# Layer 1's plain slices in six blocks of 384 tokens, attention's queries in parts of 384 and 192, the order drawn with lengthened durations

## The chip, the core and the metric

The kernel runs on one core of a Trainium2 chip. The metric is the device time of one execution in microseconds. The engines are TensorE (PE in the rows; PEld is its loading of weights), VectorE (DVE), ScalarE (ACT), GpSimd (POOL) and SyncE (SP), which issues all DMAs.

## What is computed

Attention with a threshold over 4 batches, 8 heads, 576 tokens and 64 channels, and behind it two feed-forward layers on the 2304 tokens it gives, each with an inner width of 2048:

```python
scores = scale * np.matmul(q, k.transpose(0, 1, 3, 2))
thresh = np.max(scores, axis=-1, keepdims=True) - tau
scores = np.where(scores >= thresh, scores, -1000000000.0)
attn = np.exp(scores - np.max(scores, axis=-1, keepdims=True))
attn = attn / (np.sum(attn, axis=-1, keepdims=True) + 1e-09)
x = np.matmul(attn, v)                          # to (2304, 512)
h = x @ w_in                                    # layer 1, 512 to 2048
g = np.where(h >= 1, h, np.where(h <= -1, 0.0, (h + 1) ** 2 / 4))
x = g @ w_out                                   # 2048 to 512
h = x @ w_in2                                   # layer 2
y = (s * np.maximum(h, 0) ** 2 + b) @ w_out2
```

All data are fp32, and the weights come in as fp64. Products that need the precision are done as three fp32r matmuls with a high and a low part of each factor.

## The kernel before

The program is not written in the order in which it runs. Functions `add` tasks (some instructions on one engine, or on one of several) with a duration, a priority and the buffers that they read and write; `Sched.run` plays them through with these durations and writes every engine's instructions in the order in which they began there. Each engine then works through its own list in that order and waits where a semaphore isn't set. Where the planner sees PE idle before `FILL` (200 us of its own clock) and a bank is free, it puts in a dummy matmul of the identity (L1541), which computes nothing that is used.

The work has three stages. **Attention** takes 32 units, a pair of heads and one part of a batch's queries each; a part was 256 queries (two blocks of 128 rows) or 320 (two blocks, and a mixed one with the last 64 queries of both heads). For each block of 128 queries of one head ("head-block" below): scores on PE (L587 in plain fp32 for the first two batches, L596 in fp32r from the third on), min on VectorE (L640), exp on ScalarE (L643) into a tile `p`, threshold and sum on VectorE (L648), division (L683, L678), transposes on PE (L704, L720) and their evictions (L696) into `pt` and `pl`. A tile `p` holds two head-blocks, and there are `NP` = 4 of them. When a unit's blocks are there, `av` multiplies them by the values (L742, L743): one value product for each unit, evicted into `xh` and `xl`, high and low part, and copied to `xT` in DRAM.

**Plain slices** are layer 1's first 8 of 16 slices of 128 inner channels. The tokens lay in eight blocks, two to a batch, of 256 and 320 tokens. For a block and a slice, `hidden` multiplies 12 matmuls (L937), ScalarE and VectorE shape the result (L943 to L949, L565), and `a1_out` (L970) or `l1_out` (L1018) multiplies 12 more for the output. `FB` says how many slices of a block run beside attention, as lower priority in between: 3, 7, 8, 8, 8, 8, 8 of the first seven blocks. The others (8 of the last block, 5 of the first, 1 of the second) follow attention. Weights are converted from fp64 in pieces on ScalarE, VectorE and GpSimd while attention starts.

**Passes**: the other half of layer 1, and layer 2, in three passes over three blocks of 768 tokens with a scheme that saves multiplications (`gemm1` and what follows it; L1275, L1320, L1394, L1436).

Scores use pairs of PSUM banks, three pairs up to unit `ALONE` and two from there on, when the third becomes the two banks of the slices.

Of the kernel before, what the change touches and what calls it, by code (L numbers as in the profile page):

```python
# [1 line left out]

# [5 lines left out]
F32 = mybir.dt.float32  # L8
# [16 lines left out]
FB = [3, 7, 8, 8, 8, 8, 8]  # L25
# [13 lines left out]
NP, NST, NH, LEAD = 4, 4, 3, 3  # L39
NYS = 8  # L40
# [13 lines left out]
ALONE = 7  # L54
# [40 lines left out]
HELD = float("inf")  # L95

# [33 lines left out]
class Sched:  # L130
# [241 lines left out]
def attention_then_ffn(tc, qk, v, tau, w1, w2, s2, b2, out):  # L372
# [198 lines left out]
    def scores(u, blk, x):  # L571
# [126 lines left out]

    def blocks_of_keys(u, pr, p, kp, c0, x, mixed, blk):
# [14 lines left out]
        dst = PT[:, :, :, 512:S].rearrange("p s k c -> p k s c") if mixed else PT[:, x, :, blk * 128:blk * 128 + 128]  # L714
        evict(512, pr, [dst], src, [("bank", g)], kt, g)

    def last_keys(u, pr, p, kp, mixed, blk):

        g = Group([(4,), (5,)])
        add([("pe", 109, lambda: nc.tensor.transpose(bank[g.banks[0]][:, 0:128], p[:, 512:640], ident))], at(pr, "trans"), r=kp, w=[("bank", g)] + [("PL", blk)] * (u < ALONE), group=g)  # L720
# [5 lines left out]
        c = slice(512, S) if mixed else slice(blk * 128, blk * 128 + 128)  # L726
        evict(300 if mixed else 128, pr, [PL[0:64, c], PL[64:128, c]] if mixed else [PL[:, c]], src, [("bank", g)], [("PL", blk)], g)

    def av(u, b, pair, part):
# [4 lines left out]
        c0, n = ((0, 256), (256, 320))[part]  # L734
        blks = ((0, 1), (2, 3, 4))[part]
# [59 lines left out]
    def attention():  # L795
# [8 lines left out]
        for u, (b, pair, half_) in enumerate(units):  # L804
# [3 lines left out]
            if pair == H // 2 - 1 and 2 * b + half_ < NA1:  # L808
                beside(2 * b + half_)
# [807 lines left out]
```

## Time and profile before

| | us |
|---|---|
| median of 3 runs | 1058.02 (1057.4 to 1058.94) |
| the profiled execution | 1057.3 |
| its span, first to last instruction | 1055.2 |
| PE busy | 1032.3 (98%) |
| VectorE, ScalarE, GpSimd busy | 866.8, 729.4, 493.5 |
| end of the slices, start of the passes | 502.29 |

PE is the busiest engine, but a PE record lasts longer than the step from one matmul to the next, since matmuls are pipelined; where a matmul's price matters, it is read from the chain, which counts steps, or from one start to the next. The granted clock is 1.00 of 2.4 GHz in all stretches.

### The profile page before, as it was taken

How to read it: one execution, taken by the hardware profiler on the slowest of the kernel's cores; microseconds unless marked ns; L12 is line 12 of the kernel's file. 1: busy time of each engine (PE TensorE's matmuls, PEld its weight loads, DVE VectorE, ACT ScalarE, POOL GpSimd, SP SyncE). 2: the span in 40 equal slices, each digit the busy share in tenths (PEclk: the TensorE clock that was granted, in tenths of full speed). 3: DMA queues.
4: the chain of work that ended last, by engine and by line, in shares of the span. 5: the costliest groups of instructions: out<-in, count | busy, mean ns of one | idle time of the engine just before them, and what ended most of it. 6: DMA issues, size and time to landing. Idle time of an engine off the chain costs nothing.

```text
span 1055.2 us, 20159 instructions
## 1 busy us (share of the span) xinstructions
PE 1032.3 (98%) x6772; PEld 931.7 (88%) x6772; DVE 866.8 (82%) x1786; ACT 729.4 (69%) x1418; POOL 493.5 (47%) x722
## 2 busy tenths in 40 slices
PE   8989999999999999999999999999999999999998
PEld 5556777788888889899999999998998989999998
DVE  7998998778888888755998978789998636988887
ACT  7999988988899889844553635358685636647381
POOL 5665766899998878523101513222231103424241
PEclk9999999999999999999999999999999999999999
DMA  5654555565656666389965659974968946445531
GB/s 175 184 171 147 152 171 178 168 208 159 215 160 215 198 193 206 119 288 378 343 197 208 200 194 377 333 254 161 338 224 310 381 151 208 152 133 194 174 101 61
DMA packets 117943, 221.01 MB, mean 209 GB/s; under 512 B 12752, under 2 KB 37072, under 8 KB 117840
## 3 DMA queue, kind: packets, MB, share of 16 engines
q1 hardware_dynamic: 117840, 219.73, 62.7%
q8 instruction: 54, 0.88, 0.4%
q14 instruction: 49, 0.40, 0.1%
HBM read 152.44 MB, written 67.24 MB: 208 GB/s over the span
## 4 chain that ended last, share of the span: by engine, by line
PE 71%; ACT 14%; DVE 7%; POOL 4%; issue 3%; DMA 1%; SPq 0%; POOLq 0%; DVEq 0%; ACTq 0%
PE ps L1275 25%; PE ps L1320 9%; PE ps L1436 9%; PE ps L1394 9%; ACT p L683 4%; PE ps L937 4%; PE ps L970 4%; ACT p L643 3%; PE ps L742 3%; ACT pt L696 2%; DVE p L648 2%; PE ps L1018 2%; PE ps L704 2%; PE ps L587 1%; DVE stt L640 1%
## 5 line engine op out<-in xcount | busy, mean ns | idle before, releaser
L1275 PE MATMUL ps<-pr,lr 128*128 128x384 f32 x816 | 144.2, 334 | 0.0
L1275 PEld LDWEIGHTS ps<-pr,lr 128*128 128x128 f32 x816 | 141.7, 188 | 0.0
L648 DVE SCALAR_TENSOR_TENSOR p<-ps,stt,p 128x576 f32<-128x576 f32 x144 | 115.4, 813 | 30.4 <-ACT p L643 24.7
L1275 PE MATMUL ps<-lr 128*128 128x384 f32 x672 | 121.1, 334 | 0.0
L1275 PEld LDWEIGHTS ps<-lr 128*128 128x128 f32 x672 | 116.8, 188 | 0.2
L640 DVE TENSOR_REDUCE stt<-ps 128x1 f32<-128x576 f32 x144 | 105.8, 748 | 10.4 <-PE ps L587 6.3
L937 PE MATMUL ps<-xh,lr 128*128 128x320 f32 (+1 forms) x512 | 112.2, 299 | 1.9 <-DVE lf L947 0.8
L643 ACT ACTIVATE p<-ps,stt 128x576 f32<-128x576 f32 x144 | 104.4, 746 | 7.2 <-DVE stt L640 6.3
L683 ACT ACTIVATE p<-p,stt 128x576 f32<-128x576 f32 (+3 forms) x127 | 101.7, 811 | 6.5 <-DVE stt L667 5.0
L566 DVE TENSOR_TENSOR pr<-lg,pr 128x768 fp32r<-128x768 f32 (+1 forms) x79 | 69.9, 904 | 33.3 <-PE ps L1436 17.2
L937 PEld LDWEIGHTS ps<-xh,lr 128*128 128x128 f32 x512 | 84.8, 188 | 4.2 <-DVE lf L947 2.3
L970 PE MATMUL ps<-g,lr 128*128 128x256 f32 (+1 forms) x600 | 87.1, 297 | 0.5 <-ACT lf L979 0.4
L704 PE MATMUL ps<-ident,p 128*128 128x128 f32 x576 | 82.5, 275 | 4.5 <-ACT pt L696 3.0
L1162 ACT COPY lg<-ps 128x384 f32<-128x384 f32 (+1 forms) x106 | 51.7, 491 | 50.5 <-PE ps L1275 38.9
L970 PEld LDWEIGHTS ps<-g,lr 128*128 128x128 f32 x600 | 80.4, 188 | 1.6 <-ACT lf L979 0.8
L704 PEld LDWEIGHTS ps<-ident,p 128*128 128x128 f32 x576 | 66.2, 140 | 17.2 <-ACT pt L696 4.1
L696 ACT COPY pt<-ps 128x512 f32<-128x512 f32 x140 | 78.3, 589 | 4.4 <-PE ps L704 4.0
L1436 PE MATMUL ps<-lr,pr 128*128 128x512 f32 x324 | 76.5, 389 | 0.0
L937 PE MATMUL ps<-xl,lr 128*128 128x256 f32 (+1 forms) x256 | 75.2, 294 | 0.0
L742 PE MATMUL ps<-pt,vr 128*64 128x256 f32 (+1 forms) x512 | 69.4, 412 | 3.1 <-DVE lf L947 2.5
L1436 PEld LDWEIGHTS ps<-lr,pr 128*128 128x128 f32 x324 | 60.8, 188 | 12.5
L565 POOL TENSOR_TENSOR g<-lf,g 128x256 fp32r<-128x256 f32 (+1 forms) x64 | 53.9, 844 | 35.2 <-ACT g L949 32.1
(155 smaller groups left out, 2470.4 us busy)
## 6 DMA issues: line engine op xcount, KB each, us to landing
lr<-wd SPq DMA_DIRECT2D x178, 256.0 KB, 5.3
wd<-lh SPq DMA_DIRECT2D x102, 256.0 KB, 3.8
lk<-in_w_dram SPq DMA_DIRECT2D x48, 512.0 KB, 4.9
vr<-in_v_dram SPq DMA_DIRECT2D x32, 320.0 KB, 3.4
r<-in_qk_dram SPq DMA_DIRECT2D x32, 288.0 KB, 3.1
lg<-y1T SPq DMA_DIRECT2D x6, 1536.0 KB, 8.2
lk<-in_w_dram SPq DMA_DIRECT2D x32, 256.0 KB, 3.8
wd<-pr SPq DMA_DIRECT2D x28, 256.0 KB, 4.3
```

The lines of the kernel that those rows point to most:

```text
L640: add([("dve", 665, lambda: nc.vector.tensor_reduce(out=nm[:, x:x + 1], in_=Sv(), axis=AX.XY, op=ALU.min))], at(pr, "min"), r=[kg], w=[ks[ ...
L643: add([("act", 624, lambda: nc.scalar.activation(out=ev, in_=Sv(), func=AF.Exp, bias=nm[:, x:x + 1], scale=-1.0))], at(pr, "exp"), r=[kg, ...
L648: nc.vector.scalar_tensor_tensor(out=ev, in0=Sv(), scalar=nthr[:, x:x + 1], in1=ev, op0=ALU.is_le, op1=ALU.mult, accum_out=sm[:, x:x + 1])
L683: nc.scalar.activation(out=p[i:j, o:o + w], in_=p[i:j, a:a + w], func=AF.Identity, scale=rc[i:j, x:x + 1], bias=un[i:j, x:x + 1])
L696: add([("act", actp_ns(n), lambda: [nc.scalar.copy(out=a, in_=b) for a, b in zip(dst, src())]), ("dve", dve_ns(n), lambda: [nc.vector.tens ...
L704: nc.tensor.transpose(bank[g.banks[0]][:, j * 128:(j + 1) * 128], p[:, c0 + j * 128:c0 + (j + 1) * 128], ident)
L742: nc.tensor.matmul(o[64 * x:64 * x + 64, 0:n], vr[:, c:c + D], PT[:, x, k, c0:c0 + n], start=(k == 0), stop=False)
L937: nc.tensor.matmul(o, a, x, start=(n == 0), stop=(n == 11))
L970: nc.tensor.matmul(o, a[:, c], x, start=(f == 0 and n == 0), stop=(f == nf - 1 and n == 2))
L1275: nc.tensor.matmul(o, a, y, start=(i == 0 and p in (1, 5, 2)), stop=(i == 5), skip_group_check=p not in (1, 5, 2))
L1320: nc.tensor.matmul(o, w, x, start=(f == rows[0] and s == 0), stop=(f == rows[-1] and s == 2))
L1436: nc.tensor.matmul(o, a, y, start=(f == rows[0] and s == 0), stop=(f == rows[-1] and s == 2))
```

## The change

- The tokens of two batches make three blocks of 384: the first 384 of one batch, the last 192 of both, the first 384 of the other. So there are six blocks, and `FB` has five entries: 4, 8, 8, 8, 8. Four slices of block 0 and eight of block 5 follow attention.
- A unit has 384 queries (three blocks of 128) or 192 (one block and the mixed one). In batches 1 and 3 the parts of 192 come first, so that a block of two pieces is complete early. `pt` and `pl` shrink to 384 columns, two parts of 192 side by side.
- `hidden` is two tasks of six matmuls, between which the planner may put something else (`HK`). The output was in two parts already.
- While its clock is below 460 us, the planner lengthens each duration on ScalarE, VectorE and GpSimd by a random 0 to 10% (seed `DRAW`).
- `NP` is 3 for 4, `NYS` 5 for 8, `ALONE` 6 for 7.

```diff
+HK = 2
+AK = 2
+
+TM = 384
+NQ = NT // TM
 WC = 256
 NWT = 4
 
-FB = [3, 7, 8, 8, 8, 8, 8]
+FB = [4, 8, 8, 8, 8]
...
-NP, NST, NH, LEAD = 4, 4, 3, 3
-NYS = 8
+NP, NST, NH, LEAD = 3, 4, 3, 3
+NYS = 5
...
-ALONE = 7
+ALONE = 6
...
+DRAW, SPREAD, DRAW_TO = 3, 0.1, 460000.0
...
+                    if now < DRAW_TO and e in ("act", "dve", "pool"):
+                        t.fn = (e, t.fn[1] * (1.0 + SPREAD * rnd.random()), *t.fn[2:])
...
+    YE = [ap_.tile([128, TM], F32, name=f"ye{i}") for i in range(2)]
...
-        return (0 if half_ else 256), nk, (nk if half_ else 0), (256 if not half_ else 320 if b < SPLIT else 384)
+        return (0 if half_ else TM), nk, (nk if half_ else 0), (TM if not half_ else S - TM if b < SPLIT else 256)
...
+    def col(u, blk):
+
+        return 128 * blk if not units[u][2] else (S - TM) * (units[u][1] % 2) + 128 * (blk - 3)
+
+    def pt_keys(x, c, n):
+        return [(x, i) for i in range(c // 64, (c + n) // 64)]
...
-        c0, n = ((0, 256), (256, 320))[part]
-        blks = ((0, 1), (2, 3, 4))[part]
+        n = S - TM if part else TM
+        c0 = col(u, 3 * part)
...
-    units = [(b, pair, half_) for b in range(B) for half_ in range(2) for pair in range(H // 2)]
...
+    units = [(b, pair, half_) for b in range(B) for half_ in ((1, 0) if b % 2 else (0, 1)) for pair in range(H // 2)]
+
+    def block_of(b, part):
+        return 3 * (b // 2) + (1 if part else 2 * (b % 2))
+
+    def pieces(q):
+
+        b = 2 * (q // 3)
+        return [(b * S + TM, S - TM), (b * S + S + TM, S - TM)] if q % 3 == 1 else [(b * S + S * (q % 3 // 2), TM)]
...
-        for part, blks in ((0, (0, 1)), (1, (2, 3))):
+        for part, blks in ((0, (0, 1, 2)), (1, (3,))):
...
-            if pair == H // 2 - 1 and 2 * b + half_ < NA1:
-                beside(2 * b + half_)
+            if pair == H // 2 - 1 and (b % 2 or not half_) and block_of(b, half_) < NA1:
+                beside(block_of(b, half_))
...
+        def mm(ks):
...
+        for i in range(0, 4, HK):
+            ks = range(i, i + HK)
+            add([("pe", 3 * HK * mm_ns(T), lambda ks=ks: mm(ks), "r")], pr, r=["two"] + wkeys(f, 0) + [(t, xs, j, a) for t in ("XH", "XL") for j in range(4) for a in range(2)], w=[kg, "hidden order"] + gs[0] + gs[1], group=g)
...
+            fs = range(half_ * nf // AK, (half_ + 1) * nf // AK)
...
-    blocks = [(q, 0, F1) for q in range(NA1, 2 * B)]
+    blocks = [(q, 0, F1) for q in range(NA1, NQ)]
```

What this makes of the order is seen on PE. The first place is around the 11th value product. In before, behind it (`ps_1_1128` and its like are a bank, `p_104` a tile of probabilities, `r_112` queries and keys of one head):

```order
L587 MATMUL ps_0_94<-r_112 128x288 x2
L587 MATMUL ps_1_95<-r_113 128x288 x2
L704 MATMUL ps_0_96<-ident,p_104 128x128 x4
L720 MATMUL ps_1_97<-ident,p_104 128x128
L1541 MATMUL ps_1_1128<-ident 128x128 x7
L704 MATMUL ps_0_96<-ident,p_105 128x128 x4
L587 MATMUL ps_0_94<-r_112 128x288 x2
L704 MATMUL ps_1_97<-ident,p_105 128x128 x4
L720 MATMUL ps_0_96<-ident,p_105 128x128
L587 MATMUL ps_1_95<-r_113 128x288 x2
```

And in the changed kernel, between the 10th and the 11th value product, where the lines are L1582 for the dummies, L719 and L738 for the transposes, L595 for the scores:

```order
L719 MATMUL ps_0_98<-ident,p_104 128x128 x4
L719 MATMUL ps_1_99<-ident,p_104 128x128 x4
L1582 MATMUL ps_1_1212<-ident 128x128 x12
L738 MATMUL ps_0_98<-ident,p_104 128x128
L1582 MATMUL ps_1_1212<-ident 128x128 x2
L719 MATMUL ps_1_99<-ident,p_105 128x128 x4
L595 MATMUL ps_0_96<-r_115 64x288 x2
L595 MATMUL ps_0_96<-r_116 64x288 x2
L738 MATMUL ps_0_98<-ident,p_105 128x128
L595 MATMUL ps_1_97<-r_113 128x288 x2
L1582 MATMUL ps_1_1212<-ident 128x128
L760 MATMUL ps_0_1211<-pt,vr_117 64x192 x8
```

Seven dummies stood in one run before, and 39 in the whole program; now one run has twelve, and there are 93, 92 of them ahead of the 12th value product. No slice stands in that stretch of the changed kernel.

The second place is in the third batch. Before, a hidden slice stood in one piece between transposes and scores:

```order
L720 MATMUL ps_0_96<-ident,p_103 128x128
L704 MATMUL ps_1_97<-ident,p_104 128x128 x4
L937 MATMUL ps_0_1127<-xh_73,lr 128x256
L937 MATMUL ps_0_1127<-xl_75,lr 128x256
L937 MATMUL ps_0_1127<-xh_73,lr 128x256 x2
L937 MATMUL ps_0_1127<-xl_75,lr 128x256
L937 MATMUL ps_0_1127<-xh_73,lr 128x256 x2
L937 MATMUL ps_0_1127<-xl_75,lr 128x256
L937 MATMUL ps_0_1127<-xh_73,lr 128x256 x2
L937 MATMUL ps_0_1127<-xl_75,lr 128x256
L937 MATMUL ps_0_1127<-xh_73,lr 128x256
L596 MATMUL ps_0_94<-lr 128x288 x4
```

Now (L978 is the hidden slice, L760 and L761 the value product):

```order
L978 MATMUL ps_1_1212<-xh_74,lr 128x384
L978 MATMUL ps_1_1212<-xl_76,lr 128x384
L978 MATMUL ps_1_1212<-xh_74,lr 128x384 x2
L978 MATMUL ps_1_1212<-xl_76,lr 128x384
L978 MATMUL ps_1_1212<-xh_74,lr 128x384
L760 MATMUL ps_0_1211<-pt,vr_117 64x192 x8
L761 MATMUL ps_0_1211<-pl,vr_117 128x192
L738 MATMUL ps_0_98<-ident,p_104 128x128
L719 MATMUL ps_1_99<-ident,p_105 128x128 x4
L978 MATMUL ps_1_1212<-xh_74,lr 128x384
L978 MATMUL ps_1_1212<-xl_76,lr 128x384
L978 MATMUL ps_1_1212<-xh_74,lr 128x384 x2
```

Six matmuls of a slice stand alone, then a value product and transposes, then the other six of the same sum.

## Rows read from the trace of the kernel before

**Rows 1.** Windows: length, busy PE, PEld, DVE, ACT, POOL; clock, DMA share, GB/s.

```profile
0.00:50.00 50.00, 44.14 (x284) 28.32 (x286) 42.30 (x107) 42.07 (x84) 29.35 (x74) 1.00 0.61 184
50.00:100.00 50.00, 45.07 (x321) 29.99 (x317) 45.50 (x120) 46.84 (x101) 30.42 (x64) 1.00 0.50 157
0.00:150.00 150.00, 139.05 (x953) 95.26 (x953) 134.63 (x344) 134.27 (x283) 96.13 (x205) 1.00 0.55 165
150.00:500.00 350.00, 341.25 (x2539) 301.59 (x2536) 275.77 (x665) 287.02 (x583) 261.98 (x373) 1.00 0.64 206
450.00:500.00 50.00, 49.43 (x363) 47.76 (x362) 28.23 (x55) 21.40 (x49) 16.72 (x19) 1.00 0.96 339
```

**Rows 2.** Chain that ended last, pieces in order of time: start, us, what.

```profile
21.36 1.88 PE ps L742 x16
...
28.32 0.69 PE ps L587 x4
...
71.55 2.30 PE ps L742 x16
...
74.59 0.44 PE ps L704 x4
...
138.19 1.88 PE ps L742 x16
...
142.56 1.56 PE ps L1541 x14
...
204.18 2.80 PE ps L970 x24
...
455.53 7.08 PE ps L937 x48
...
502.29 28.09 PE ps L1275 x162
```

**Rows 3.** The same chain from 0 to 150 us, shares by line.

```profile
by line: PE ps L742 11.8%; PE ps L937 10.4%; PE ps L587 9.8%; ACT p L683 9.5%; PE ps L704 8.9%; ACT pt L696 7.4%; ACT p L643 6.9%; PE ps L1541 5.3%; DMA lk<-in_w_dram 4.4%; issue 3.9%; PE ps L743 3.9%; ACT lk L879 2.1%; DVE stt L640 1.4%; D
```

**Rows 4.** Timeline of PE: start, us, instructions in a run, idle before and releaser.

```profile
1.34 2.50 PE L790 MATMUL ps<-ident 128*128 128x128 f32 x10 [1.34 <-POOL ident masks.py:199]
...
7.13 2.39 PE L1541 MATMUL ps<-ident 128*128 128x128 f32 x18
9.46 1.24 PE L587 MATMUL ps<-r 64*128 64x288 f32 x8
...
14.08 0.33 PE L720 MATMUL ps<-ident,p 128*128 128x128 f32 x1 [0.63 <-ACT pt L696]
...
23.17 0.70 PE L743 MATMUL ps<-pl,vr 128*128 128x256 f32 x2
23.70 0.60 PE L704 MATMUL ps<-ident,p 128*128 128x128 f32 x4
24.23 1.24 PE L587 MATMUL ps<-r 64*128 64x288 f32 x8
...
73.78 0.81 PE L743 MATMUL ps<-pl,vr 128*128 128x320 f32 x2
74.43 0.60 PE L704 MATMUL ps<-ident,p 128*128 128x128 f32 x4
...
289.67 0.78 PE L596 MATMUL ps<-lr 128*128 128x288 f32 x4
...
290.83 0.27 PE L720 MATMUL ps<-ident,p 128*128 128x128 f32 x1
```

**Rows 5.** Groups of instructions by form: busy us, mean ns of one, idle before.

```profile
L1541 PE MATMUL ps<-ident 128*128 128x128 f32 x78 | 12.4, 292 | 1.4 <-ACT pt L696 1.0 <-ACT lf L979 0.4
...
L945 ACT ACTIVATE lf<-lf,cst 128x320 f32<-128x320 f32 x32 | 17.9, 564 | 13.9 <-DVE lf L943 13.7
...
L945 ACT ACTIVATE lf<-lf,cst 128x256 f32<-128x256 f32 x32 | 16.2, 507 | 3.1 <-DVE lf L943 3.0
```

**Rows 6.** Timeline of ScalarE: the first two exps.

```profile
6.38 1.45 ACT L643 ACTIVATE p<-ps,stt 128x576 f32<-128x576 f32 x2
```

More of the change, by code (lines that the diff above doesn't have):

```diff
@@ L719, in last_keys @@
         g = Group([(4,), (5,)])
-        add([("pe", 109, lambda: nc.tensor.transpose(bank[g.banks[0]][:, 0:128], p[:, 512:640], ident))], at(pr, "trans"), r=kp, w=[("bank", g)] + [("PL", blk)] * (u < ALONE), group=g)
+        at_, m = col(u, blk), 64 if mixed else 128
+        kl = pt_keys("PL", at_, m)
+        add([("pe", 109, lambda: nc.tensor.transpose(bank[g.banks[0]][:, 0:128], p[:, 512:640], ident))], at(pr, "trans"), r=kp, w=[("bank", g)] + kl * (u < ALONE), group=g)
         def src():
@@ L743, in mm @@
             nc.tensor.matmul(o[:, 0:n], vr[:, 8 * D:8 * D + 128], PL[:, c0:c0 + n], start=False, stop=True)
-        rd = ["two"] * (u >= ALONE) + [("VR", u % NV)] + [("PT", x, t) for x in range(2) for t in blks] + [("PL", t) for t in blks]
-        q = 2 * b + part
-        t0, c = b * S + c0, slice(pair * n, pair * n + n)
-        xh, xl, kh, kl = XH[q % 2][:, c], XL[q % 2][:, c], ("XH", q % 2, pair), ("XL", q % 2, pair)
-        add([("pe", value_ns(n), mm)], at(pr, "av"), r=rd, w=[kg, kh, kl], group=g)
+        rd = ["two"] * (u >= ALONE) + [("VR", u % NV)] + [k for t in ("PT0", "PT1", "PL") for k in pt_keys(t, c0, n)]
@@ L751, in av @@
+        q, parts = block_of(b, part), (b % 2,) if part else (0, 1)
+        t0, c = b * S + TM * part, pair * TM + (S - TM) * (part and b % 2)
+        xh, xl = XH[q % 2][:, c:c + n], XL[q % 2][:, c:c + n]
+        kh, kl = ([(t, q % 2, pair, a) for a in parts] for t in ("XH", "XL"))
+        add([("pe", value_ns(n), mm)], at(pr, "av"), r=rd, w=[kg] + kh + kl, group=g)
         add([("act", actp_ns(n), lambda: nc.scalar.copy(out=xh, in_=bank[g.banks[0]][:, 0:n])),
              ("dve", dve_ns(n), lambda: nc.vector.tensor_copy(out=xh, in_=bank[g.banks[0]][:, 0:n]))],
-            at(pr, "xo"), r=[kg], w=[kh], group=g)
+            at(pr, "xo"), r=[kg], w=kh, group=g)
@@ new lines, in columns, with shaped_as, among, x_keys @@
+    def columns(t, q):
+        b = 2 * (q // 3)
+        if q % 3 == 1:
+            return t[:, b * S:b * S + 2 * S].rearrange("p (a c) -> p a c", a=2)[:, :, TM:S]
+        return t[:, pieces(q)[0][0]:pieces(q)[0][0] + TM]
+    def shaped_as(y, q):
+        return y.rearrange("p (a c) -> p a c", a=2) if q % 3 == 1 else y
+    def among(t0, T):
+        return [q for q in range(NQ) if any(a < t0 + T and a + w > t0 for a, w in pieces(q))]
+    def x_keys(qs, x):
+        return [("xT", q, p, x, a) for q in qs for p in range(H // 2) for a in range(2)]
@@ L1179, in load_x @@
         keys = [("y1", t0, dm, a) for dm in range(4) for a in ((0,) if dm < 3 or T <= 512 else (0, T // 2))]
-        qs = [q for q in range(2 * B) if span(q)[0] < t0 + T and sum(span(q)) > t0]
+        qs = among(t0, T)
         if P.layer == 1:
-            keys = [("xT", q, p, 0) for q in qs for p in range(H // 2)]
+            keys = x_keys(qs, 0)
         add([("sp", DMA_ISSUE, lambda: nc.sync.dma_start(out=x_b(0, 4 * T).rearrange("p (k t) -> p k t", k=4), in_=rows_of(src)))],
@@ L1304, in gemm2_across @@
         rows = P.rows()
-        qs = [q for q in range(2 * B) if span(q)[0] < t0 + T and sum(span(q)) > t0]
+        qs = among(t0, T)
         def at_(dm, a):
@@ L1485, in hid @@
         q, f0, _ = blocks[k]
-        T = span(q)[1]
+        T = TM
         gs[n] = gslot(n % NGL, T)
         hidden(f, T, (k + NA1) % 2, ANY, gs[n])
-        if f == f0 + 1 and 2 * B - NA1 <= k + 1 < len(blocks):
+        if f == f0 + 1 and NQ - NA1 <= k + 1 < len(blocks):
             load_parts(blocks[k + 1][0], (k + 1 + NA1) % 2)
```

100 lines of the change are left out of this document (48 added, 52 removed).

## The prediction

> **What bounds the kernel now.** I read the table of windows first [rows 1]; the reader is to see how little of TensorE (PE) is free. It is idle for 150 - 139.05 = 10.9 us up to 150 us, mostly in the first 100, and for 350 - 341.25 = 8.8 us from there to 500: in all 19.7. At 50 to 100 us ScalarE has 46.84 and VectorE 45.50 of 50 busy, PE 45.07: attention runs nearly alone there and nobody is idle for long.
>
> Then the chain that ended last [rows 2]. From 502.29 us on it is matmuls of the passes, to the end of the span (1055.2): 552.9 us, which the change doesn't touch. From 455.53 to 502.29 it is slices alone, dense. So everything is decided before 502.29, and before that by what PE has to do and what it waits for. The third view is the share of the lines in the chain up to 150 us [rows 3]: 5.3% of it, 8.0 us, are matmuls of L1541, the dummies that the planner puts where its own plan shows PE idle. They take their time on the path, and whatever stands behind them waits.
>
> **A ledger of PE up to 502.29 us.** A slice's matmul takes 2.80 / 24 = 0.1167 us for 256 tokens and 7.08 / 48 = 0.1475 for 320 [rows 2]; 768 of each make 89.6 + 113.3 = 202.9. A value product takes 1.88 us (256 queries) or 2.30 (320), and its last matmul 0.53 or 0.65 (23.17 to 23.70, 73.78 to 74.43) [rows 2, 4]: 16 of each, 66.9 + 18.9. Transposes: 0.44 for four [rows 2], so 656 x 0.11 = 72.2. Scores in plain fp32: 0.69 a group of four records [rows 2], 80 groups, 55.2. Scores in fp32r: eight in 1.16 us (289.67 to 290.83) [rows 4], 320 of them, 46.4. Dummies: 18 records from 7.13 to 9.46, 0.129 each [rows 4]; there are 78 records (39 matmuls) [rows 5], 10.1. Warm-up 2.5 [rows 4]. Sum 475.1; **the rest**, 27.2 us, is the 19.7 of idle time and 7.5 of switches and waits too short to show.
>
> **The change part by part.**
>
> Six blocks of 384. A matmul of 384 tokens stands in the passes: 28.09 / 162 = 0.1734 us [rows 2]. 1152 of them make 199.7: **-3.2 us**. The gain is that a token costs 0.451 ns at 384 against 0.456 and 0.461. The Trainium skill (TensorE: Matmul & The Clock Gate, section Back-to-back issue gap) has a rule that speaks for less: a warm gap of N / 2.4 ns plus a fixed 2.5. By it only 384 fixed parts would go, the term would be -1.0 and the sum end at 1057, no change. The rows differ from it (0.1167 where it gives 0.109), and the sum goes by the rows.
>
> Where the slices lie moves too. Before, 27 slices of 256 and 23 of 320 run beside attention, 75.6 + 81.4 = 157.0 us, and 45.9 are left. Now 36 of 384 run beside it (149.8) and 12 after it (49.9). That is in the -3.2 already; it says only that the dense stretch at the end grows by 4.0.
>
> Queries in 384 and 192. Value products are linear between the two rows, 0.42 us for 64 queries, so 2.72 + 1.46 = 4.18, as 1.88 + 2.30 before; the last matmuls likewise. Scores, transposes, exps, masks and evictions are as many as before. **Nothing**. The ACT and DVE work of the slices falls with their number, 64 to 48: the square takes 564 ns for 320 and 507 for 256 [rows 5], so 279 ns of it don't depend on the width, and 16 x 0.28 = 4.5 us leave ScalarE, beside PE. It shortens waits at most; if ScalarE were the bound it would be a gain of up to 4.5, and I leave it out.
>
> DMAs: xT and ypT go out in as many bytes, a block of two pieces in two loads. The DMA share is 0.55 up to 150 us, and 0.96 from 450 to 500 [rows 1], but the slices there follow each other without a wait. So nothing, as long as the loads of block 0 come before its turn; 8 slices of block 5 (33 us) lie ahead of it on PE. Without that cover a load would cost what it takes to land, a few us.
>
> The third pair of banks for scores is given up one unit earlier (`ALONE` 6 for 7): three head-blocks with one score less in flight, between nothing and about 1 us (the length of a score and its min), nearer to nothing because slices stand in the same banks then.
>
> Slices in two turns. A hidden slice may be left after six matmuls. A switch to fp32 scores costs about 0.09 us (23.70 to 24.23 is 0.53, four transposes being 0.44) [rows 2, 4]. The order has 271 switches before and 307 now: 36 x 0.09 = 3.2 at most. I take it inside the rest.
>
> Lengthened durations. The planner believes ScalarE, VectorE and GpSimd to be up to 10% slower, 5% in the mean. Two effects. First, where PE has no slice it plans more idle time and fills it: 93 dummies for 39, 108 more records, **+13.9 us**. 92 of the 93 stand ahead of the 12th value product; block 0 now has four slices where blocks 0 and 1 had ten begun, so five units of attention run with no slice beside them. Second, engines that are faster than planned come early, and PE waits less. Bounds for the rest: 27.2 if nothing shrinks; about 6 if only the start (1.34) and a few switches stay. Break-even with 475.1 - 3.2 + 13.9 = 485.8 is 502.3 - 485.8 = 16.5.
>
> Which value? By legs. Up to its 11th value product (138.19 [rows 2]) before has done 48 head-blocks of attention (128 queries of one head), 72 slice matmuls of 256 and 93 of 320 (8.4 + 13.7 = 22.1 us) and 31 dummies (8.0). After needs 12 value products for the same 48, with 96 matmuls of 384 (16.6) and 92 dummies (23.7): 138.19 - 22.1 - 8.0 + 16.6 + 23.7 = 148.4 with the idle time of before. But gaps such as the 0.63 us at 14.08, where a transpose waits for an eviction [rows 4], are what the dummies fill. I leave 3.4 of the 10.9 for the start (1.34) and stray waits: 140.9. In the second leg I halve the 8.8 (-4.2) and take 2.0 off the 7.5, for the margin of 5%; both are choices, nearer to the lower bound since 8.0 of 10.1 us of dummies lay on the path already. The slices left there are 183.1 for 180.8, the dummies 0.3 for 2.1: 364.1 + 2.3 - 1.8 - 4.2 - 2.0 = 358.4. Pass start 499.3: **-3.0 us**, the rest at 13.5.
>
> The profiled execution took 1057.3 us with a span of 1055.2; the sum gives 1054.3. The median of the runs shown is 1058.0, 0.7 above, so I say 1055.0.
>
> **The rivals.**
>
> Slower: the dummies stay on the path and buy nothing. PE takes its instructions in order; a transpose whose probabilities are ready stands behind up to 12 dummies in a row. The 8.0 of 10.1 us that lie on the chain before [rows 3], and 14 records at 142.56 with no wait behind them [rows 2], speak for it. Against it: some of that time would be idle without them. If the waits of the second leg stay and only half of the first leg's go, the rest is 22: +5.5, about 1063.5; with nothing gained (27.2) 1068.7. It decides from a rest of 18.6.
>
> Slower too: three probability tiles (P) instead of four. Early on 12 tiles take 71.55 - 21.36 = 50.2 us, 4.2 each; three of them give a tile 12.5 us from its exp to its last transpose. The first one took 6.38 to 14.08 + 0.33, 8.0 us, on an empty machine [rows 4, 6]. At a life of 14 us each tile costs 0.5 us more, 28 tiles 14 us, part of it where dummies lie anyway: about 1064. It would be the exps on ScalarE that wait, and behind them in its queue the evictions that free the transposes' banks.
>
> No change: the rest falls to 14.4 to 18.6, and the gain in waits pays for the dummies, no more; 1058. It needs only that I halved the waits of the second leg without right.
>
> More: the second leg runs nearly dry and the first is held by nothing but PE: rest 7, 1049.
>
> The clock: five units without slices could bring PE to 1.2 GHz, 15 head-blocks of (138.19 - 22.1 - 8.0 - 10.9) / 48 = 2.0 us, twice as long less the dummies there, an estimate of 20 us, 1078. Rows speak against it: the granted clock is 1.00 in the first 50 us, where PE has no slice at all [rows 1]. The same page of the Trainium skill (Part 4: PE-mode transpose) says that transposes don't count as busy for the clock; the first stretch doesn't bear that out.
>
> That it does not do what it says can be left out: the order shows the six blocks and the dummies.
>
> **How the numbers follow.** A measurement of this kernel can tell about 0.2% (2.1 us) from no change. Forecast (rest 10 to 14.4) 0.34; more (below 10) 0.10; no change 0.24; dummies 0.24; P tiles 0.06; clock 0.02. So faster 0.44, same 0.24, slower 0.32. The range runs from a rest near 6 (1048) to 24 (1066) and leaves out the clock and the worst of the dummies. The forecast alone: 1051.5 to 1055.9.
>
> **What would show it.** Right: 186 records of L1582, about 24 us; the 12th value product near 141 us with idle time below 4 us up to there; L978 and L1011 at 0.173 us each; dense slices for 50 us up to a first pass matmul near 499; passes of 552.9 us as before. Wrong: the 12th value product at 145 us or later, or idle time of PE between 150 and 450 us that is still 8 us; then the slower cases hold. A pass stretch that changes in length would break the frame of the sum.

## The result

The changed kernel takes 1063.82 us (median of 4 runs, 1062.95 to 1063.86), the kernel before 1057.8 beside it: a ratio of 1.0054 with an interval of 1.0042 to 1.0066. It is **slower by 6 us**, where 1055.0 was forecast; the range ended at 1066. The profiled execution has a span of 1062.0 us for 1055.2.

The chain that ended last (start, us, what), at the 12th value product and from the dense slices on:

```profile
131.88 2.68 PE ps L1582 x24
...
147.04 1.45 PE ps L760 x16
...
457.47 8.33 PE ps L978 x48
...
499.64 8.48 PE ps L1059 x48
508.12 29.14 PE ps L1316 x168
537.26 33.28 PE ps L1361 x192
```

And of the kernel before, the piece that answers to the last one:

```profile
530.38 9.71 PE ps L1320 x56
```

The 12th value product begins at 147.0, where 140.9 was forecast and 145 named as the sign of the slower cases. At the second run of pass matmuls the difference is 537.26 - 530.38 = 6.88 us, and it stays that to the end: the passes are as long as before, and everything is lost ahead of them. (In the chain the run of pass matmuls begins at 508.12 for 502.29 [rows 2], but in the kernel before six of its matmuls, 1.04 us, were already done ahead of the last slice: 162 for 168.)

The windows (length, busy PE, PEld, DVE, ACT, POOL with instructions, granted clock, DMA share, GB/s), as [rows 1] had them:

```profile
0.00:150.00 150.00, 142.57 (x973) 98.92 (x974) 123.31 (x327) 126.02 (x262) 87.79 (x185) 1.00 0.54 161
150.00:500.00 350.00, 344.33 (x2204) 298.47 (x2203) 280.29 (x627) 281.27 (x544) 269.72 (x386) 1.00 0.61 195
450.00:500.00 50.00, 49.01 (x280) 46.22 (x279) 31.59 (x50) 22.80 (x46) 17.87 (x20) 1.00 0.97 343
```

PE is idle for 7.4 us up to 150 and for 5.7 from there to 500, together 13.1 for 19.7. So the idle time did fall. But up to 150 us ScalarE and VectorE have 126.02 and 123.31 busy where they had 134.27 and 134.63 [rows 1]: attention got less done (52 exps have begun by then where 56 had) while PE looked fuller. What fills it are the dummies. Their group, and the chain's shares up to 150 us:

```profile
L1582 PE MATMUL ps<-ident 128*128 128x128 f32 x186 | 29.2, 294 | 0.9 <-ACT ye L1020 0.6 <-ACT pt L704 0.2
```

```profile
by line: PE ps L595 17.5%; PE ps L1582 15.1%; PE ps L760 13.2%; PE ps L719 9.5%; PE ps L978 5.2%; PE ps L1011 5.2%; PE ps L761 4.5%; ACT pt L704 4.0%; DMA r<-in_qk_dram 3.9%; ACT p L651 3.8%; issue 3.5%; ACT p L691 2.4%; PE ps L738 2.2%; AC
```

15.1% of 150 us, 22.6, for 8.0 before [rows 3].

**The ledger, measured.** Here each PE record is counted from its start to the start of the next one (or to its own end, where PE then idles), summed over the trace up to the passes, without those six early matmuls:

| us | before | after | difference | forecast |
|---|---|---|---|---|
| slices | 208.9 | 208.3 | -0.6 | -3.2 |
| dummies | 11.1 | 26.1 | +15.0 | +13.9 |
| idle | 19.7 | 13.1 | -6.6 | -11.7 |
| transposes, scores, value products, warm-up | 261.5 | 260.6 | -0.9 | -2.0 (short waits) |
| sum | 501.1 | 508.0 | +6.9 | -3.0 |

Each entry is rounded by itself. Against the forecast the sum is 9.9 too high: 5.1 of it is idle time that did not go, 2.6 slices that gained less, 1.1 dummies that are dearer and 1.1 other work. Put another way, PE spends 39.1 us on nothing (dummies and idle time) where it spent 30.8; its useful work is 1.5 us shorter.

**Where it is lost.** Batches 0 to 3 have 36 head-blocks each, with one exp for each, and both kernels take the batches in turn. So the start of the 36th, 72nd, ... exp marks the same count of head-blocks in both. What lies between, and the part of it that is not slices:

| stretch | before: us, slices, rest | after: us, slices, rest | rest |
|---|---|---|---|
| batch 0 | 92.2, 6.2, 86.0 | 92.6, 9.5, 83.1 | -2.9 |
| batch 1 | 103.5, 38.5, 65.0 | 112.5, 30.5, 82.0 | **+17.0** |
| batches 2 and 3 | 245.0, 110.9, 134.1 | 240.6, 114.1, 126.5 | -7.6 |
| last exp to the passes | 60.4, 53.3, 7.1 | 62.2, 54.2, 8.0 | +0.9 |

Everything is lost in batch 1, and nearly half of it comes back in batches 2 and 3. Not all of the 17.0 is a loss, though: dummies are 10.7 of it, idle time 0.7 and scores and transposes 1.8, but 3.5 are value products which in the kernel before come behind the 72nd exp, and which batches 2 and 3 have 3.7 less of now. In dummies and idle time alone, which no such shift touches, batch 1 has 16.2 us for 4.8 and batches 2 and 3 have 4.7 for 7.6.

The closest look is at twelve head-blocks at the same place of the count, from the start of the 42nd exp to that of the 54th: 106.8 to 143.8 us before and 119.2 to 153.2 after. Of before, all engines, then PE's records of the hidden slices (L937) and of the output (L970):

```profile
106.80:143.80 37.00, 37.00 (x266) 29.61 (x266) 35.49 (x91) 33.06 (x73) 26.77 (x48) 1.00 0.54 152
...
106.80:143.80 37.00, 13.35 (x84) 12.35 (x84) 1.00 0.54 152
...
106.80:143.80 37.00, 1.48 (x9) 1.36 (x9) 1.00 0.54 152
```

Of after, all engines, the hidden slices (L978) and the dummies (L1582); of the output there is no record:

```profile
119.20:153.20 34.00, 34.00 (x275) 26.10 (x275) 28.66 (x77) 28.44 (x65) 22.77 (x45) 1.00 0.62 182
...
119.20:153.20 34.00, 1.77 (x10) 1.86 (x11) 1.00 0.62 182
...
119.20:153.20 34.00, 11.26 (x84) 10.26 (x84) 1.00 0.62 182
```

With 14.0 us of slices and 2.3 of dummies beside it (start to start) attention took 37.0; with 1.8 us of slices it takes 34.0, and 10.1 us of dummies stand in their place. The twelve are not the same blocks: now more of them are mixed, and PE's own part of attention is 22.2 us for 20.6. Still, 12.2 us of slices less make the stretch only 3.0 us shorter. Work that cost little beside attention is missing there, and stands at other places now (batch 0 +3.3, batches 2 and 3 +3.2, the end +0.9). In the trace such a place looks like this (PE, start, us, a run of instructions):

```profile
130.79 1.09 PE L719 MATMUL ps<-ident,p 128*128 128x128 f32 x8
131.72 2.84 PE L1582 MATMUL ps<-ident 128*128 128x128 f32 x24
134.40 0.27 PE L738 MATMUL ps<-ident,p 128*128 128x128 f32 x1
134.51 0.61 PE L1582 MATMUL ps<-ident 128*128 128x128 f32 x4
134.95 0.60 PE L719 MATMUL ps<-ident,p 128*128 128x128 f32 x4
```

These are the twelve dummies in one run that the order showed. PE is never idle here, and 28 records, 3.1 us at 0.112 (2.68 / 24 in the chain), are of no use to anyone.

### The profile page after: what moved, and what is told of

Read it like the earlier page. It is cut to its first block, busy times and chain, and to the rows that moved or that the text cites. A ratio compares the mean times of both kernels' runs of the same rounds, so it can differ in the third digit from the quotient of the medians.

```text
span 1062.0 us, 19475 instructions
## 1 busy us (share of the span) xinstructions
PE 1045.8 (98%) x6496; PEld 939.1 (88%) x6496; DVE 867.9 (82%) x1733; ACT 721.6 (68%) x1371; POOL 497.2 (47%) x730
## 4 chain that ended last, share of the span: by engine, by line
PE 84%; ACT 7%; DVE 4%; issue 2%; POOL 2%; DMA 1%; SPq 0%; POOLq 0%; ACTq 0%; DVEq 0%
PE ps L1316 25%; PE ps L1361 9%; PE ps L1477 9%; PE ps L1435 9%; PE ps L978 8%; PE ps L760 4%; PE ps L1011 4%; PE ps L719 4%; PE ps L595 4%; PE ps L1059 2%; PE ps L1582 2%; PE ps L604 2%; ACT p L651 2%; ACT p L691 1%; PE ps L761 1%
## 5 line engine op out<-in xcount | busy, mean ns | idle before, releaser
L1316 PE MATMUL ps<-pr,lr 128*128 128x384 f32 x816 | 144.2, 334 | 0.0
L656 DVE SCALAR_TENSOR_TENSOR p<-ps,stt,p 128x576 f32<-128x576 f32 x144 | 116.0, 811 | 23.0 <-ACT p L651 20.6
L648 DVE TENSOR_REDUCE stt<-ps 128x1 f32<-128x576 f32 x144 | 106.9, 750 | 28.0 <-PE ps L604 14.4
L978 PE MATMUL ps<-xh,lr 128*128 128x384 f32 x384 | 111.2, 346 | 0.1
L691 ACT ACTIVATE p<-p,stt 128x576 f32<-128x576 f32 (+3 forms) x108 | 87.9, 822 | 10.5 <-DVE stt L675 9.6
L704 ACT COPY pt<-ps 128x512 f32<-128x512 f32 x139 | 77.6, 591 | 11.7 <-PE ps L719 11.2
L719 PE MATMUL ps<-ident,p 128*128 128x128 f32 x576 | 81.0, 275 | 4.5 <-ACT pt L704 2.2
L1011 PE MATMUL ps<-g,lr 128*128 128x384 f32 x432 | 82.5, 340 | 0.9 <-DVE lf L985 0.9
L719 PEld LDWEIGHTS ps<-ident,p 128*128 128x128 f32 x576 | 65.9, 140 | 17.4 <-ACT pt L704 4.7
L1011 PEld LDWEIGHTS ps<-g,lr 128*128 128x128 f32 x432 | 74.0, 188 | 2.2 <-DVE lf L985 1.4
L978 PEld LDWEIGHTS ps<-xh,lr 128*128 128x128 f32 x384 | 70.7, 189 | 2.0 <-DVE lf L989 1.0
L760 PE MATMUL ps<-pt,vr 128*64 128x384 f32 (+1 forms) x512 | 69.4, 412 | 0.1
L573 POOL TENSOR_TENSOR g<-lf,g 128x384 fp32r<-128x384 f32 x48 | 50.2, 1046 | 34.3 <-ACT g L991 33.4
L889 ACT CAST pr<-lf 128x384 fp32r<-128x384 f32 (+1 forms) x50 | 28.5, 582 | 53.8 <-DVE lf L574 19.0
```

The lines of the kernel that those rows point to most:

```text
L648: add([("dve", 665, lambda: nc.vector.tensor_reduce(out=nm[:, x:x + 1], in_=Sv(), axis=AX.XY, op=ALU.min))], at(pr, "min"), r=[kg], w=[ks[ ...
L656: nc.vector.scalar_tensor_tensor(out=ev, in0=Sv(), scalar=nthr[:, x:x + 1], in1=ev, op0=ALU.is_le, op1=ALU.mult, accum_out=sm[:, x:x + 1])
L691: nc.scalar.activation(out=p[i:j, o:o + w], in_=p[i:j, a:a + w], func=AF.Identity, scale=rc[i:j, x:x + 1], bias=un[i:j, x:x + 1])
L719: nc.tensor.transpose(bank[g.banks[0]][:, j * 128:(j + 1) * 128], p[:, c0 + j * 128:c0 + (j + 1) * 128], ident)
L760: nc.tensor.matmul(o[64 * x:64 * x + 64, 0:n], vr[:, c:c + D], PT[:, x, k, c0:c0 + n], start=(k == 0), stop=False)
L978: nc.tensor.matmul(o, a, x, start=(k == 0 and n == 0), stop=(k == 3 and n == 2))
```

## The experiments

My theory after the comparison: the blocks of 384 leave a long part of batch 1 without slices (block 0 has four of them beside attention, and block 1 is complete only when batch 1's parts of 192 are), and the dummies only fill what is left empty. The rivals: the dummies themselves delay attention; three tiles of probabilities hold it; the lengthened durations drew a bad order. "Rest of batch 1" below is the 65.0 and 82.0 of the table. In the labels, a is the changed kernel and b the kernel before.

### The dummies left out

```diff
-WARM, WARM_NS, FILL_FROM = 5, 1917.0, 4500.0
+WARM, WARM_NS, FILL_FROM = 5, 1917.0, 300000.0
```

> The changed kernel with every instruction in its order, only the dummies are not issued (186 records, 26.0 us from start to next start). Theory 1, the dummies lie on the path and delay what stands behind them: most of the time comes back, PE's idle time up to the 12th value product grows from 7.4 us to no more than 20, the 12th value product comes at 134 to 141 instead of 147.0, the median is 1050 to 1057. Theory 2, they only fill time in which PE would wait anyway (for ScalarE, VectorE, or a probability tile): the 12th value product stays at 146 to 148, idle time there is 30 us or more, the median 1062 to 1065. Theory 3, they hold the clock up: a granted clock under 1.00 in the first 150 us and a median above 1068.

> The same edit in the kernel before: its 78 dummy records (11.1 us) are not issued, all else in the same order. Theory 1: the 11th value product moves from 138.2 to 130 to 135, the median is 1051 to 1055. Theory 2: 138 as before, idle time up to there 19 to 22 us instead of 11.0, the median 1057 to 1059. Theory 3: clock under 1.00 and a median above 1060.

Measured: 1059.49 us (ratio to before 1.0014, interval 1.0005 to 1.0023) for the changed kernel, and 1057.05 (0.9991, 0.9981 to 1.0) for the one before. 26.1 us of dummies give back 4.3 us, 11.1 of them 0.9. The first leg (up to the 12th value product) of the changed kernel without dummies, windows and the chain's piece at its end:

```profile
0.00:50.00 50.00, 42.95 (x231) 24.28 (x233) 40.92 (x105) 42.43 (x84) 27.05 (x68) 0.93 0.54 163
...
100.00:150.00 50.00, 44.19 (x305) 30.40 (x305) 41.00 (x110) 40.78 (x92) 34.32 (x68) 0.93 0.67 195
```

```profile
140.96 2.11 PE ps L760 x11
```

The 12th value product comes at 140.9 for 147.0. Of the 25.7 us of dummies that stood there, 12.4 come back as idle time (7.4 to 19.8); scores and transposes take 6.2 us more, with a granted clock of 0.93 in the first 50 us and from 100 to 150; and 6.1 are saved. So theory 1 had this leg right and the median not; about half of the dummies fill waits, some hold the clock, and about a quarter delays. In the kernel before, the 11th value product comes at 136.9 with 15.6 us of idle time, between theories 1 and 2.

Only the late ones, in a version of the last loop:

```diff
-            if t.start >= FILL_FROM or t.alts:
+            if FILL_FROM <= t.start < 90000.0 or t.alts:
```

> The changed kernel with the dummies left out that the planner puts behind its 90th us (57 of 93, about 16 of 26.0 us, nearly all in batch 1); those ahead of it stay. All else in the same order. If batch 1's dummies delay what stands behind them: batch 1 (112.5 us) loses 5 us or more, the median 1056 to 1060. If they only fill waits, or hold the clock there: batch 1 at 110 to 112.5, idle time of PE there up from 1.8 to 10 or more, the median 1061 to 1064.

1061.55 (1.0035, 1.0022 to 1.0048). Batch 1 takes 110.2 us for 112.5, with no dummy and 8.7 us of idle time: 14.4 us of dummies were worth 2.3. The clock shows what they do besides. Windows of 4 us, columns as above:

```profile
128.00:132.00 4.00, 1.68 (x13) 1.00 (x9) 3.85 (x11) 3.66 (x7) 3.13 (x6) 1.00 0.80 264
132.00:136.00 4.00, 3.92 (x25) 2.12 (x27) 3.78 (x10) 3.61 (x11) 2.56 (x6) 0.71 0.72 190
...
140.00:144.00 4.00, 2.27 (x17) 1.17 (x17) 3.67 (x10) 3.62 (x11) 3.54 (x7) 0.99 0.24 82
144.00:148.00 4.00, 4.00 (x23) 2.23 (x20) 3.57 (x10) 2.35 (x5) 2.38 (x5) 0.58 0.23 70
```

PE is busy for 1.68 of 4 us, and behind that the clock of 2.4 GHz goes to 1.2 for a part of the next stretch; the same twice. With the dummies it was 1.00 all the way. The Trainium skill (TensorE: Matmul & The Clock Gate, Part 4: PE-mode transpose) says that transposes don't count as PE-busy in the same way for the clock. PE had transposes, plain fp32 scores and value products here, and idle time between them, so these rows agree with it and don't prove it. What the prediction held against it, a clock of 1.00 in the first 50 us of before, does not hold: that stretch had dummies, and without them its clock is 0.93.

### The want of slices, alone

```diff
-FB = [3, 7, 8, 8, 8, 8, 8]
+FB = [3, 1, 8, 8, 8, 8, 8]
```

> The kernel before with one slice of block 1 beside attention instead of seven (FB 3, 1, 8, ... for 3, 7, 8, ...); the other six follow attention. 73 dummies for 39. It gives the old layout the new one's want of slices while batch 1 begins, and nothing else of the change. In the new layout batch 1 (from its first exp to its last) takes 82.0 us besides its slices, dummies 14.4 of them, in the old 65.0 with 3.7. If the want of slices is the cause: that number rises to 72 to 82 here, dummies there to 10 or more, and the median to 1062 to 1069. If the slices just move to the end and attention goes as much faster: about 65 us and 1057 to 1060; the cause then lies in the units of 384 and 192 or in the order drawn.

1068.02 (1.01, 1.0083 to 1.0117). The rest of batch 1 is 71.7 us, just under the 72 to 82 of the theory, with 8.3 us of dummies where it wanted 10, and the median is 10.2 us up. The windows of batch 1 and of the time from the last exp to the passes, and that last one in the kernel before:

```profile
92.10:193.10 101.00, 98.69 (x740) 73.48 (x740) 91.36 (x236) 90.04 (x194) 74.75 (x137) 1.00 0.57 175
430.50:511.40 80.90, 79.77 (x580) 77.07 (x577) 55.80 (x111) 40.20 (x86) 24.09 (x30) 1.00 0.88 297
```

```profile
440.70:501.10 60.40, 59.83 (x446) 57.34 (x443) 33.32 (x68) 28.54 (x64) 18.97 (x23) 1.00 0.89 315
```

Attention ends 10.2 us earlier (430.5 for 440.7) with 20 us fewer slices beside it, and those take 20.5 us more at the end. That is the price of a slice that leaves attention: about half.

In the changed kernel the want can be made larger, with batch 1's units in the plain order, 384 ahead of 192, so that the next block is complete later:

```diff
-    units = [... for half_ in ((1, 0) if b % 2 else (0, 1)) ...]
+    units = [... for half_ in ((1, 0) if b == 3 else (0, 1)) ...]
```

> The changed kernel with batch 1's units in the plain order, 384 before 192, so that the second block of slices to be complete comes after six head-blocks a pair instead of three; 139 dummies for 93. If the want of slices decides: more of it, 3 to 10 us more (1067 to 1074), dummies in batch 1 beyond 14.4 us. If the mixed blocks in front decide: 1057 to 1063.

1089.13 (1.0297, 1.0279 to 1.0314), more than any theory said. The chain's shares in batch 1, here, in the changed kernel and in the kernel before:

```profile
by line: PE ps L1582 20.3%; PE ps L595 18.3%; PE ps L760 15.3%; PE ps L719 14.4%; PE ps L978 11.5%; PE ps L1011 7.7%; PE ps L761 4.6%; PE ps L738 2.8%; DVE p L656 1.2%; ACT p L651 1.1%; ACT p L691 0.7%; PE ps L604 0.7%; DVE lf L989 0.5%; is
```

```profile
by line: PE ps L595 20.5%; PE ps L760 15.1%; PE ps L978 14.8%; PE ps L719 13.9%; PE ps L1582 12.2%; PE ps L1011 10.0%; PE ps L761 5.0%; PE ps L738 3.7%; ACT pt L704 1.0%; ACT p L691 0.8%; ACT p L651 0.7%; issue 0.5%; ACT lf L987 0.5%; ACT y
```

```profile
by line: PE ps L937 13.6%; ACT p L683 12.6%; PE ps L587 9.8%; PE ps L704 8.5%; ACT p L643 8.0%; PE ps L742 7.3%; PE ps L970 6.0%; ACT pt L696 5.8%; issue 4.9%; DVE p L648 4.0%; PE ps L1541 3.7%; PE ps L743 2.4%; ACT pl L696 1.5%; ACT lk L87
```

Dummies are 20.3, 12.2 and 3.7% of the chain there (24.1, 13.7 and 3.8 us), and the rest of batch 1 is 93.2, 82.0 and 65.0. They go together with the longest stretch of batch 1 in which PE has no record of a slice: 66.1, 39.0 and 16.9 us, and in the run with `FB` 1 26.0, where the rest is 71.7. Of the changed kernel (L978, the same for L1011), then of the kernel before (L937, the same for L970):

```profile
112.60:151.30 38.70, 0.00 (x0) 0.00 (x0) 1.00 0.63 185
```

```profile
135.00:151.60 16.60, 0.00 (x0) 0.00 (x0) 1.00 0.51 144
```

Behind batch 1 this kernel lost more still, 14 us of its 25 (idle time 16.4 us in the second leg for 5.7), which I have not followed.

That the mixed blocks come first in batch 1 was tried in the old layout:

```diff
-    units = [(b, pair, half_) for b in range(B) for half_ in range(2) for pair in range(H // 2)]
+    units = [(b, pair, half_) for b in range(B) for half_ in ((1, 0) if b == 1 else (0, 1)) for pair in range(H // 2)]
```

> The kernel before with batch 1's parts of 320 queries ahead of those of 256 (the change's own order of batch 1, done alone); 49 dummies for 39. Batch 1 besides its slices: 65.0 us in the old layout, 82.0 in the new one, and 71.7 where the old one only lacks slices there. If mixed blocks that come first are the rest of it: 70 to 77 us here and a median of 1060 to 1066. If their place doesn't matter: 64 to 68 and 1056 to 1060.

1068.61 (1.0101, 1.0084 to 1.0118), slower than either case said, and the rest of batch 1 at 69.4, between the two. It adds 4.4 us there; the other six of the loss are spread over batch 2 (+2.6), the end (+3.3) and dearer slices (+2.7), less 3.1 in batch 3. This order, too, makes the longest stretch of batch 1 without a slice longer, 26.8 us for 16.9, so it need not be a cause apart from the want of slices. Of the 17.0 us of batch 1, fewer slices show 6.7 and the order of the parts 4.4 in the old layout. In dummies and idle time alone, batch 1 has 4.8 us before, 10.6 with `FB` 1, 9.3 here and 16.2 in the changed kernel; whether the two parts add up was not tried in one run.

### Three tiles of probabilities

```diff
-NP, NST, NH, LEAD = 4, 4, 3, 3
+NP, NST, NH, LEAD = 3, 4, 3, 3
```

> The kernel before with three tiles of probabilities instead of four, nothing else; 41 dummies for 39. If three tiles hold attention back (the second slower rival): exps start later, the 11th value product comes at 144 to 150 instead of 138.1, the median is 1063 to 1072. If not: 137 to 141 and 1056 to 1060.

1062.83 (1.0048, 1.0033 to 1.0063), just under the rival's range, and the 11th value product at 144.8 for 138.1, as the rival said. The granted clock is 0.93 from 50 to 100 us there, where it was 1.00; how much of this is the clock and how much the wait for a tile was not told apart. In the changed kernel a fourth tile fits where two of the slices' g buffers go (`NP` 4, `NGA` 6); its counterpart has `NGA` 6 alone:

> The changed kernel with four tiles of probabilities instead of three; the room is taken from the slices' g buffers (six for eight, NGA). 97 dummies for 93. Three tiles cost the old layout 6.6 us up to its 11th value product (138.1 to 144.7). If it is the tiles that make the new layout's first leg longer: the 12th value product at 138 to 142 instead of 147.0 and a median of 1056 to 1060, unless the missing g buffers cost as much later. If it is the missing slices (the layout): 145 to 148, the median as that of the same kernel with three tiles and six g buffers, within 2 us.

> The counterpart: the changed kernel with six g buffers and its three tiles; 103 dummies. First leg 145 to 148 by every theory (only four slices run there). What it takes longer than 1063.8 is what six g buffers cost in the second leg: 0 to 5 us.

1072.53 (1.0138, 1.0119 to 1.0156) with four tiles and 1063.29 (1.005, 1.0032 to 1.0068) with three. The 12th value product comes at 144.2 and 146.3. So the tiles are 2 to 3 us of the first leg in the new layout, not the 9 by which its mark lies later than the old one's, and the order with four loses 10.3 us in the second leg, by a cause that I have not looked for: neither outcome that I had written down.

### The lengthened durations

Left out of the changed kernel, added alone to the one before, and each with another draw:

```diff
-DRAW, SPREAD, DRAW_TO = 3, 0.1, 460000.0
+DRAW, SPREAD, DRAW_TO = 3, 0.0, 460000.0
```

> The changed kernel planned with the plain durations (spread 0 for 0.1). Its order has 86 dummies for 93. If the lengthened durations are what costs time (the prediction put all new dummies down to them): 1056 to 1060. If the layout is (blocks of 384 leave PE without a slice while the first five units run): 1061 to 1065, with the 12th value product at 145 to 148. If the lengthening is worth what the prediction hoped, idle time in the second leg rises from 5.7 to 8 us or more and the median to 1065 to 1068.

> The kernel before, planned with the lengthened durations of the change and nothing else of it. Its order has 53 dummies for 39, 28 records more, 3.9 us at 0.14. If dummies cost their time and the waits stay: 1060 to 1062. If the lengthening takes away waits as the prediction had it (second leg 4 to 6 us less): 1054 to 1057. If it does nothing that can be told: 1057 to 1059.

> The changed kernel with another draw of the lengthened durations (seed 1 for 3), nothing else; its order has 99 dummies for 93. So far the draw of seed 3 takes 6.4 us from the new layout (1070.2 to 1063.8) and adds 5.5 to the old one (1057.9 to 1063.5). Theory A, lengthening as such shortens the waits of the new layout: 1061 to 1066, idle time of PE in the second leg 5 to 7 us. Theory B, every draw is another order, and the spread between orders is some 5 us whatever the layout: anything between 1060 and 1073, and beyond 1066 or under 1061 about as likely as not.

> The kernel before with lengthened durations of seed 1; 51 dummies for 39 (53 with seed 3). Theory A for the old layout (lengthening costs it its dummies and the early clock): 1061 to 1066. Theory B: anything between 1055 and 1066. If the granted clock from 50 to 100 us is 1.00 here (it was 0.90 with seed 3), and the time 1057 to 1060, the loss of seed 3 was that place and not the dummies.

| us | plain durations | seed 3 | seed 1 |
|---|---|---|---|
| old layout | 1057.8 | 1063.46 (ratio 1.0036 to 1.0066) | 1057.73 (0.9993 to 1.0013) |
| new layout | 1070.2 (1.0103 to 1.0133) | 1063.82 (1.0042 to 1.0066) | 1065.7 (1.0061 to 1.0094) |

The new layout is slower by 12.4 us with plain durations and by 8.0 with seed 1; with seed 3 the 0.4 us lie within the noise. Batches 1 and 2 together show the layout more steadily: their rest is 145.8, 145.0 and 145.1 us in the new one and 132.1, 136.2 and 127.3 in the old one. Which of the two batches has it depends on the draw: with seed 1 the changed layout has 39.7 us of slices in batch 1, more than the kernel before, and still 36.0 us without any in one stretch, a rest of 76.1 there and 68.9 in batch 2. Two runs lie beyond all that I had written down for them: 1070.2, and 1063.46 in the old layout. The new layout's dummies are there without the lengthening (86 for 93), so my putting them down to it was wrong. What the lengthening gives the new layout lies in the second leg, as predicted: 369.5 us plain, 361.0 and 363.8 with it (idle time 9.0, 5.7 and 7.8). In the old layout seed 3 loses its 5.5 us at the start: the 11th value product comes at 144.4, with the clock at 0.90 from 50 to 100 us; with seed 1 it is 0.97 there, and 140.6. Between two draws of one layout lie 1.9 and 5.7 us: as much as the change itself.

### The two turns of a hidden slice

One task of twelve in the changed kernel, with seed 3 and with seed 1, and two tasks of six in the kernel before:

```diff
-HK = 2
+HK = 4
```

> The changed kernel with a hidden slice in one task of twelve matmuls, as in the kernel before, instead of two of six; 95 dummies for 93. If the splitting costs its switches (slices take 189.6 us in the second leg where 1056 matmuls at 0.1745 make 184.3): slices there 187 to 188.5, the median 1061 to 1063. If the two turns are worth something in waits: idle time in the second leg rises from 5.7 to 8 or more, the median 1065 to 1069.

> A second draw (seed 1) of the changed kernel with hidden slices in one task of twelve, against 1065.7 for two tasks of six with that seed; 104 dummies for 99. In the first draw one task cost 17.6 us. If that is what the long task does: 1075 or more. If most of it was that one order: 1063 to 1071. Old layout: the splitting brought nothing (1058.2 for 1057.7).

```diff
-        add([("pe", 12 * mm_ns(T), mm, "r")], pr, ...
+        for i in range(0, 4, 2):
+            ks = range(i, i + 2)
+            add([("pe", 6 * mm_ns(T), lambda ks=ks: mm(ks), "r")], pr, ...
```

> The kernel before with its hidden slices in two tasks of six matmuls, one part of the change done alone. In the new layout one task of twelve took 17.6 us more than two of six (1081.4 to 1063.8), 17.2 of it behind the 12th value product, with 9.6 us more idle time. If that is what a long task does (12 x 0.1745 = 2.1 us in which PE serves no score and no transpose; 1.4 or 1.8 us in the old layout): a gain here too, smaller, 1050 to 1056. If it was the order drawn, nothing sure: 1055 to 1063. If the splitting only costs switches (0.09 us each, 20 more at most): 1058 to 1060.

1081.42 (1.0223, 1.0208 to 1.0238) and 1075.45 (1.0167, 1.0151 to 1.0182), 17.6 and 9.8 us more than with two turns, the first beyond both of its cases; in the old layout 1058.2 (1.0003, 0.9994 to 1.0013), no difference, where a gain had been the first case. The loss lies in batches 2 and 3, in the second draw in batch 3 alone (rest 69.5 for 60.3). In the first of these two kernels, batch 2 and batch 3:

```profile
217.00:337.30 120.30, 113.19 (x718) 97.87 (x719) 94.44 (x223) 103.25 (x204) 102.29 (x146) 0.99 0.55 173
337.30:462.70 125.40, 118.81 (x780) 105.02 (x780) 107.19 (x235) 111.10 (x217) 103.00 (x138) 0.97 0.62 193
```

and of the changed kernel:

```profile
205.20:326.40 121.20, 119.36 (x777) 104.68 (x776) 93.38 (x218) 102.16 (x199) 104.10 (x156) 1.00 0.57 176
326.40:445.80 119.40, 116.57 (x787) 104.08 (x786) 100.08 (x232) 105.39 (x205) 103.85 (x143) 1.00 0.56 175
```

PE idles for 7.1 and 6.6 us where it idled for 1.8 and 2.8, with 11 us fewer slices done (103.0 for 114.1), and the clock falls a little. A hidden slice of 384 in one piece is 12 x 0.1745 = 2.1 us; that scores come too late behind it is what I argued, and the runs show the idle time, not that chain.

### A version that beats both

The old layout with two turns and a lengthened draw (seed 14), without the rest of the change:

> The old layout with two of the change's parts, two tasks of six and lengthened durations (seed 14), and not the others; 46 dummies for 39. The draws of the old layout so far gave 1057.7, 1057.7, 1058.2 and 1063.5. If lengthening helps the margin of waits once no blocks of 384 starve PE: 1052 to 1056. If the draws scatter around the plain order or above it: 1057 to 1064.

1055.81 us, ratio 0.9981 (0.9972 to 0.9991): 2 us faster than the kernel before, 8 faster than the changed one. Batches 2 and 3:

```profile
200.90:311.60 110.70, 109.30 (x816) 97.93 (x816) 91.51 (x226) 98.68 (x207) 96.46 (x130) 1.00 0.59 178
311.60:427.30 115.70, 114.64 (x863) 102.20 (x863) 95.08 (x240) 104.96 (x212) 100.56 (x144) 1.00 0.55 175
```

2.5 us of idle time in these two batches, where the kernel before has 7.6. Its seed was picked from some fifty orders (seeds 0 to 24, with and without the two turns) by where the planner's own plan ended, before any of them had run. So it shows that such an order exists, not that a draw finds one by itself.

## Why the prediction was wrong

- **What bounds it, and the frame**: right. (The first leg is the time up to the 11th or 12th value product, the second what follows up to the passes.) PE alone decides, up to the passes, which didn't change. The sum of the rest came out at 508.1 - 485.8 = 22.3 where I took 13.5, 18.6 was the turning point, and the slower rival had 22 and 1063.5.
- **Idle time of the first leg**: the step that failed most, 4.0 of the 9.9 us. I wrote that gaps are what the dummies fill, and took idle time from 10.9 to 3.4. It is 7.4, and the leg is 147.0 for 140.9 (dummies +2.0, slices +2.0, idle time +4.0, other work less). Behind it stands the deeper mistake: I moved the first leg to equal head-blocks, took out the slices that no longer stood there, and let attention go faster by all of their time. Attention does not: beside 14.0 us of slices twelve head-blocks took 37.0 us, beside 1.8 us twelve take 34.0. That five units have no slice beside them stood in the prediction, and was priced as dummies alone, not as lost cover.
- **Lengthening as the source of the dummies**: wrong. They come with the layout; lengthening adds 7 of the 54 to it, and 12 to 14 to the old one. A record costs 0.140 us where I took 0.129.
- **Idle time of the second leg** 8.8 to 4.6: measured 5.7. Right in kind; the rest of batches 2 and 3 fell by 7.6, but 3.7 of it is value products that now come before the 72nd exp.
- **Slices at 0.1734, -3.2**: mis-sized. Where a slice's matmul has slices on both sides, the mean is 117.2 ns for 256 tokens, 146.8 for 320 and 174.5 for 384, so 768 x (0.1172 + 0.1468) - 1152 x 0.1745 = 1.7 us of gain. By the formula of the Trainium skill (TensorE: Matmul & The Clock Gate, Back-to-back issue gap), which the page gives for a matmul by itself and not for a stream of weight loads and matmuls, this term is an estimate of 1.0, and its warm gaps come to 109.2, 135.8 and 162.5 ns: the levels are off, the difference was nearer than mine. The rest, 1.1, went to the ends of the runs of slices: a first slice matmul behind transposes takes 0.261 us (48 of them), 0.087 more than inside; first matmuls together cost 5.1 us beyond their plain price for 4.8 before, last ones 2.1 for 1.3. I had left that "inside the rest".
- **Value products, transposes, scores**: as predicted, nothing (with the warm-up -0.9; value products alone -1.7, transposes +1.2).
- **P tiles**: rightly small for this layout (2 to 3 us of the first leg), though the old one lost 5 with three tiles, at a lower clock.
- **Clock**: 1.00 throughout, as predicted; by the dummies, as the runs without them show.
- **The rival that came true** named a time within 0.3 us, but by half of its mechanism: "buy nothing" holds, while leaving them out gives back only 4.3 of 26. What costs is the work that isn't there.

## What to carry to other kernels

When blocks get larger, ask first when the first and the second of them are complete, and what the busiest engine does until then; filler that lies beside a chain of waits costs less than its own time there (20 us of slices taken away shortened attention by 10), and moved elsewhere it costs all of it. A rise of busy share by dummies is no gain: count useful work between two marks that are the same in both kernels, such as the n-th exp, and look at what work has moved across them. And where an order is drawn by a planner, time several draws before a few us are put down to the idea behind a change.

## What was not expected of the hardware

- Dummies that compute nothing held the granted clock at 1.00; without them it was 0.93 in the first 50 us and from 100 to 150, and scores and transposes of the first leg took 71.7 us for 65.5.
- A matmul of 384 tokens among slices takes 174.5 ns, in the passes 173.4; the first one behind a transpose 261.
